# Score matmuls of a head pair on the two 64-row halves of TensorE, in a sliding-window attention with a multiplicative FFN

## The chip, the cores and the metric

One NeuronCore of one Trainium2 chip. The metric is the device time of one execution in microseconds (us), the median of several runs. Lower is better.

## What is computed

The reference runs attention over 8 batches, 8 heads, 576 positions and 64 values a head, with a causal window of 64 positions, and feeds the result to a feed-forward network whose hidden part is a product of two projections:

```python
scores = scale * np.matmul(q, k.transpose(0, 1, 3, 2))
rel = pos[:, None] - pos[None, :]
mask = (rel >= 0) & (rel < 64)
scores = np.where(mask, scores, -1e9)
scores = scores - np.max(scores, axis=-1, keepdims=True)
attn = np.exp(scores); attn = attn / (np.sum(attn, axis=-1, keepdims=True) + 1e-09)
attn_out = np.matmul(attn, v)
x = attn_out.transpose(0, 2, 1, 3).reshape(4608, 512)
a = x @ w1; b = x @ w2              # 512 -> 1024 each
out = ((a * b) @ w3) @ w_out        # 1024 -> 1024 -> 512
```

Inputs and output are float32; the kernel works in float16 with float32 accumulation.

## The kernel before, in words

**Weights.** `w3 @ w_out` is folded once into `wc_sb` (`fold_t`, `fold_mm`), so that the FFN is two projections (`ffn_ab`, L385) and one output matmul (`ffn_o`, L410). There are 9 groups of 512 tokens; each has 8 `ffn_ab` steps (two projections of 4 matmuls of 512 columns, cut in two where the ring of `xT` wraps) and 4 `ffn_o` steps (8 matmuls each).

**Attention.** Heads are taken in pairs: head `2j` lies on partitions 0 to 63 and head `2j+1` on 64 to 127 (`NJ` = 4 pairs). For each batch, Q and K are loaded by SyncE, cast to float16 (`cast_qk`), and transposed on TensorE in three chunks `c` of six 128x128 tiles (`transposes`, L246; the transposes are at L255, the copies out of PSUM at L262). K goes to `kT` with one copy of 128 partitions for each chunk. Q goes to `qT`, which holds for each pair two blocks: block `a` has head `a` on its 64 partitions and zeros on the other 64. The zeros are written once (L493, L494), and each chunk of Q needs two copies of 64 partitions, one on ScalarE (`a` = 0) and one on VectorE (`a` = 1).

`scores(d)` (L272) is one of six steps of a batch: three query segments `si`, two halves `jp` of the four pairs. It multiplies a 128-row block of K by the zero-padded Q of both heads at once (L282): the contraction runs over all 128 rows, of which the zeros take half. `s_ps` has two PSUM banks, one for each pair `jj`, with one buffer. ScalarE takes the exponential into `pt` (L287), and GpSimd cuts the window out of it with two `affine_select` passes (L296, L298). `values(d)` (L302) multiplies by V (L317, with columns of ones for the sums), ScalarE makes the reciprocal by logarithm and exponential (L326, L327, L329), and VectorE scales into `xT` (L332, L333).

**Order.** The order is written out by hand (a manual schedule). Lines 488 to 540 start up: loads, dummy matmuls[...] (`keep_busy`), K and Q of batch 0. Lines 542 to 566 interleave the attention of batch 0 with the fold. Lines 567 to 612 do the attention of batch 1 with FFN group 0 and prepare batch 2. From L617 on, a list of FFN steps with due times is worked through, and `tick(u)` (L362) puts scores, transposes, values, casts and loads of batches 2 to 7 between them; `late` (L341) says at which tick each chunk of the next batch is transposed. In the start-up and for batches 1 and 2 the chunks of a transpose go into spare views of `s_ps`, two in one tile, and into `tp`; later each goes into `tp`, which has one buffer.[...]

The functions that the change touches are `transposes`, `scores` and `values`, the start-up that writes the zeros, and the call for Q of batch 0.

Of the kernel before, what the change touches and what calls it, by code (L numbers as in the profile page):

```python
# [8 lines left out]
FP32 = mybir.dt.float32  # L9
FP16 = mybir.dt.float16  # L10
I32 = mybir.dt.int32
ALU = mybir.AluOpType
AF = mybir.ActivationFunctionType
PSUM = bass.MemoryType.PSUM

P = 128
SHIFT = 4.0
# [127 lines left out]
def kernel(  # L145
# [11 lines left out]
    nc = tc.nc  # L157
    B, H, S, D = q.shape
# [3 lines left out]
    scale = 1.0 / (D ** 0.5)  # L162
    NJ = H // 2
    TP, TI = 32, 18
# [7 lines left out]
    ident16 = keep.tile([P, P], FP16)  # L172
# [7 lines left out]
    const = fast.enter_context(tc.tile_pool(name="const", bufs=1))  # L180
    sb = fast.enter_context(tc.tile_pool(name="sb", bufs=2))
    ps_t = fast.enter_context(tc.tile_pool(name="ps_t", bufs=1, space=PSUM))
    ps_s = fast.enter_context(tc.tile_pool(name="ps_s", bufs=1, space=PSUM))
# [4 lines left out]
    dve_cp = nc.vector.tensor_copy  # L188
    act_cp = nc.scalar.copy
# [4 lines left out]

    v16s = [const.tile([P, 6, NJ, 4 * D], FP16, name=f"v16_{i}") for i in range(2)]

    qTs = [const.tile([P, NJ, 2, S], FP16, name=f"qT_{i}") for i in range(2)]


    raws, k16s, q16s = {}, {}, {}  # L200

# [16 lines left out]
    def cast_third(b, which, c, cp):  # L218
        t = raws[which, b]
        if c == 0:  # L220
            (k16s if which == "k" else q16s)[b] = sb.tile([P, TI, P], FP16, name=which + "16", bufs=1)
        t16 = (k16s if which == "k" else q16s)[b]
        cp(t16[:, 6 * c:6 * c + 6].rearrange("p i (hh d) -> p hh i d", hh=2),
           t[:, :, 6 * c * D:6 * c * D + 6 * D].rearrange("p hh (i d) -> p hh i d", d=D))
# [16 lines left out]
            dve_cp(vh[D:P, 1], vh[0:D, 2])  # L241


    kTs = {}

    def transposes(b, which, *cs, into=None, order=None):  # L246

        if cs[0] == 0 and which == "k":
            kTs[b] = sb.tile([P, NJ, S], FP16, name="kT")
        t16 = (k16s if which == "k" else q16s)[b]  # L250
        if into is None:
            into = [ps_t.tile([P, 6, P], FP16, name="tp")]
        for c, tp in zip(cs, into):
            for i in range(6):
                nc.tensor.transpose(tp[:, i, :], t16[:, 6 * c + i, :], ident16)  # L255

        def move(c, tp, a, cp):
            src = tp.rearrange("q i (p j) -> q j p i", p=TP)
            part = slice(0, P) if a is None else slice(a * D, a * D + D)
            dst = kTs[b] if a is None else qTs[b % 2][:, :, a, :]  # L260
            dst = dst[part].rearrange("q j (p i) -> q j p i", i=TI)
            cp(dst[:, :, :, 6 * c:6 * c + 6], src[part])  # L262

        if order is None:
            order = [(c, None, dve_cp) for c in cs] if which == "k" else \
                [(c, a, cp) for c in cs for a, cp in ((0, act_cp), (1, dve_cp))]
        for c, a, cp in order:
            move(c, into[cs.index(c)], a, cp)

    probs, lns = {}, {}  # L270

    def scores(d):  # L272
        b, r = divmod(d, 6)
        si, jp = divmod(r, 2)
        kT, qT = kTs[b], qTs[b % 2]
        seg = SEGS[si]
        w = 2 * sum(blk[2] for blk in seg)
        s_ps = ps_s.tile([P, 2, 512], FP32, name="s_ps")
        for jj in range(2):
            c0 = 0  # L280
            for (k0, q0, n, _) in seg:
                nc.tensor.matmul(s_ps[:, jj, c0:c0 + 2 * n].rearrange("k (a n) -> k a n", a=2),  # L282
                                 kT[:, 2 * jp + jj, k0:k0 + P], qT[:, 2 * jp + jj, :, q0:q0 + n],
                                 start=True, stop=True, skip_group_check=True)
                c0 += 2 * n
        pt = sb.tile([P, 2, 512], FP16, name="pt", bufs=3)
        nc.scalar.activation(pt[:, :, 0:w], s_ps[:, :, 0:w], AF.Exp, bias=-SHIFT, scale=scale)  # L287

        for (lo, hi, n, off, step) in [(0, 256, 128, 0, 0), (256, 384, 64, 64, 0)] if si == 0 else [(0, 512, 128, 64, -64)]:
            nb = (hi - lo) // (2 * n)  # L290
            sl = pt[:, :, lo:hi]
            if nb == 1:
                pat = [[0, 2], [0, 2], [1, n]]
            else:
                pat = [[0, 2], [step, nb], [0, 2], [1, n]]
            nc.gpsimd.affine_select(out=sl, in_=sl, pattern=pat, compare_op=ALU.is_ge,  # L296
                                    fill=0.0, base=off, channel_multiplier=-1)
            nc.gpsimd.affine_select(out=sl, in_=sl, pattern=[[-s, m] for s, m in pat], compare_op=ALU.is_ge,  # L298
                                    fill=0.0, base=63 - off, channel_multiplier=1)
        probs[d] = pt  # L300

    def values(d):  # L302
        b, r = divmod(d, 6)
        si, jp = divmod(r, 2)
        j0 = 2 * jp
        v16 = v16s[b % 2]
        pt = probs.pop(d)
        seg = SEGS[si]
        q_base = seg[0][1]
        o_ps = ps_v.tile([P, 2, 512], FP32, name="o_ps")  # L310
        for jj in range(2):
            first = True
            for a in range(2):
                c0 = 0
                for bi, (k0, q0, n, _) in enumerate(seg):
                    o0 = a * 192 + q0 - q_base
                    nc.tensor.matmul(o_ps[:, jj, o0:o0 + n],  # L317
                                     v16[:, si * 2 + bi, j0 + jj, a * D:a * D + P],
                                     pt[:, jj, c0 + a * n:c0 + a * n + n],
                                     start=first, stop=(bi == 1), skip_group_check=True)  # L320
                    first = False
                    c0 += 2 * n
        if jp == 0:
            lns[b, si] = sb.tile([P, NJ, 192], FP32, name="ln_s", bufs=4)
        y = lns[b, si][:, j0:j0 + 2]
        nc.scalar.activation(y[0:D], o_ps[D:P, :, 0:192], AF.Ln)  # L326
        nc.scalar.activation(y[D:P], o_ps[0:D, :, 192:384], AF.Ln)  # L327
        r = sb.tile([P, 2, 192], FP32, name="r")
        nc.scalar.activation(r, y, AF.Exp, scale=-1.0)  # L329
        x0 = (b * S + q_base) % RING  # L330
        xs = xT[:, j0:j0 + 2, x0:x0 + 192]
        nc.vector.tensor_tensor(xs[0:D], o_ps[0:D, :, 0:192], r[0:D], ALU.mult)  # L332
        nc.vector.tensor_tensor(xs[D:P], o_ps[D:P, :, 192:384], r[D:P], ALU.mult)  # L333
# [28 lines left out]
    def tick(u):  # L362

        b, r = divmod(u, 12)
        d = u // 2
        if u % 2 == 0 and d < ND:
            scores(d)
        ev = late.get(r, [])
        for e in ev:
            if e[0] == "t":  # L370
                event(b, *e)
        if u % 2 == 1 and 12 <= d - 1 < ND:
            values(d - 1)
        for e in ev:
            if e[0] != "t":
                event(b, *e)
        n, m = divmod(u - LAG - 4, 4)
        if m == 3 and n >= 6:
            keep_sums(n)
# [83 lines left out]
    rows = 2 * 3 * B  # L463
# [17 lines left out]
    def keep_busy(n):  # L481

        d = ps_t.tile([P, P], FP32, name="tp")
        for _ in range(n):
            nc.tensor.matmul(d, ident16, ident16, start=True, stop=True)
# [3 lines left out]
    load_qk(0, "q")  # L489
    nc.scalar.preload_act_table_set("natural_log_exp_and_others")  # L490
    make_identity(nc, ident16)
    for qT in qTs:
        nc.vector.memset(qT[D:P, :, 0, :], 0.0)  # L493
        nc.vector.memset(qT[0:D, :, 1, :], 0.0)  # L494

    def ones_of(i):
        nc.gpsimd.memset(v16s[i].rearrange("p c j (a e) -> p (c j a) e", a=2)[:, :, D:2 * D], 1.0)  # L497
# [17 lines left out]
    def spare(pool, name):  # L515

        t = pool.tile([P, 2, 1024], FP16, name=name)
        return [t[:, i, 0:768].rearrange("p (i n) -> p i n", i=6) for i in range(2)]

    keep_busy(75)  # L520
    tps = spare(ps_s, "s_ps") + spare(ps_v, "o_ps")
    for c in range(3):
        cast_third(0, "k", c, act_cp if c == 1 else dve_cp)
    transposes(0, "k", 0, 1, 2, into=tps, order=[(0, None, dve_cp), (1, None, act_cp), (2, None, dve_cp)])
    keep_busy(10)
    for c in range(3):
        cast_third(0, "q", c, act_cp if c == 1 else dve_cp)
    tps = [tps[3], ps_t.tile([P, 6, P], FP16, name="tp"), spare(ps_s, "s_ps")[0]]
    transposes(0, "q", 0, 1, 2, into=tps, order=[(0, 0, act_cp), (1, 1, dve_cp), (2, 0, act_cp), (0, 1, dve_cp),
                                                 (1, 0, act_cp), (2, 1, dve_cp)])  # L530
    keep_busy(15)
    scores(0)
    keep_busy(10)
    scores(1)
    keep_busy(30)
    for i in range(2):
# [50 lines left out]
    for d in range(6, 11):  # L587
# [10 lines left out]
        else:  # L598
            which, hh = [("k", 0), ("k", 1), ("q", 0), ("q", 1)][d - 7]
# [19 lines left out]
    for g in range(1, NG):  # L619
        part = [lambda g=g, fc=fc: ffn_ab(g, fc) for fc in range(8)] + \  # L620
               [lambda g=g, t=t: ffn_o(g, t) for t in range(4)]
        lo = need[g]
        hi = need[g + 1] if g + 1 < NG else NU
# [57 lines left out]
```

## Time and profile before

| | |
|---|---|
| time, median of 3 runs | 299.63 us (299.23 to 300.56) |
| span of the profiled execution | 298.8 us |
| TensorE matmul busy | 275.5 us (92%) |
| VectorE busy | 198.0 us (66%) |
| ScalarE busy | 178.4 us (60%) |
| GpSimd busy | 182.3 us (61%) |
| score matmuls (L282) | 192, 27.4 us busy |
| copies of Q out of PSUM (L262) | 24 on VectorE of about 960 ns, 24 on ScalarE of about 800 ns |
| exponentials of the scores (L287) | 48, 45.6 us |
| mask passes (L296, L298) | 128, 105.9 us |

A row of the groups' table names the line, the engine, the operation and the tiles; then how often it ran, its busy time, the mean duration of one, and how long its engine had been idle before it and for whom. Matmuls are pipelined: the recorded duration of one is longer than the time until the next one starts, and it is the distance between starts that says what a matmul costs TensorE.

### The profile page before, as it was taken

Reading aid. Unit: us, or ns where it says so; the run is one execution under the profiler, and the core shown is the slowest. Engines: PE = TensorE matmul, PEld = TensorE weight load, DVE = VectorE, ACT = ScalarE, POOL = GpSimd, SP = SyncE. Lnnn points to the kernel's source line nnn. Section 1 sums busy time; section 2 is a strip of 40 time slices with the busy share of each in tenths; the row PEclk is TensorE's granted clock in tenths of the full one; section 3 lists DMA queues with packets and bytes.
Section 4 is the critical chain, followed back from the end, with each engine's and each line's share of the span. In section 5 each row is a group of like instructions: output and inputs, shape, how many; then the busy total and the mean of one; then the engine's idle time right before and its main releaser. Section 6 shows DMA issues by size and latency. Waiting matters only on the chain.

```text
span 298.8 us, 5570 instructions
## 1 busy us (share of the span) xinstructions
PE 275.5 (92%) x2062; PEld 163.3 (55%) x2062; DVE 198.0 (66%) x302; ACT 178.4 (60%) x296; POOL 182.3 (61%) x214
## 2 busy tenths in 40 slices
PE   7578989798779999999999999999999999999992
PEld 7454645444535555555555798555556555544440
DVE  6816677565866776768767866589668756545531
ACT  2523784676447757787777756487769866641300
POOL 8746994578637956698669653795696453411200
PEclk9999999999989999999999999999999999999997
DMA  6999999990184936586819480970096012002012
GB/s 249 205 178 201 279 259 243 368 78 35 72 309 202 63 53 233 193 54 128 288 76 88 139 311 3 114 112 1 0 140 84 2 71 73 0 35 110 0 50 97
DMA packets 51663, 38.82 MB, mean 130 GB/s; under 512 B 38784, under 2 KB 41856, under 8 KB 51632
## 3 DMA queue, kind: packets, MB, share of 16 engines
q0 software_dynamic: 41744, 9.96, 36.1%
q1 hardware_dynamic: 9888, 28.46, 26.1%
q8 instruction: 17, 0.28, 0.4%
q14 instruction: 14, 0.11, 0.1%
HBM read 38.80 MB, written 9.44 MB: 161 GB/s over the span
## 4 chain that ended last, share of the span: by engine, by line
PE 72%; DVE 8%; ACT 7%; issue 4%; DMA 4%; POOL 3%; POOLq 0%; ACTq 0%
PE f_ps L401 36%; PE f_ps L414 19%; PE o_ps L317 7%; PE s_ps L282 5%; DMA ab<-in_moe_w_dram 4%; PE tp L255 3%; DVE xT L333 2%; ACT ln_s L327 2%; ACT r L329 2%; PE f_ps L460 2%; POOL v L497 2%; DVE kT L262 1%; DVE qT L262 1%; DVE xT L332 1%; ACT qT L262 1%
## 5 line engine op out<-in xcount | busy, mean ns | idle before, releaser
L401 PE MATMUL f_ps<-xT,w_sb 128*128 128x512 f16 (+1 forms) x640 | 135.5, 360 | 1.6 <-ACT a_sb L406 0.9
L296 POOL TENSOR_SCALAR_AFFINE_SELECT pt<-pt 128x512 f16<-128x512 f16 (+1 forms) x64 | 52.8, 825 | 72.7 <-ACT pt L287 72.7
L401 PEld LDWEIGHTS <-w_sb 128*128 128x128 f16 x640 | 60.6, 98 | 52.6 <-issue 3.6
L414 PE MATMUL f_ps<-wc_sb,ab 128*128 128x512 f16 x288 | 67.1, 379 | 0.1
L407 DVE TENSOR_TENSOR ab<-f_ps,a_sb 128x512 f16<-128x512 f32 x72 | 49.7, 691 | 19.0 <-PE f_ps L401 15.7
L287 ACT ACTIVATE pt<-s_ps 128x1024 f16<-128x1024 f32 (+1 forms) x48 | 45.6, 950 | 24.9 <-PE s_ps L282 24.1
L298 POOL TENSOR_SCALAR_AFFINE_SELECT pt<-pt 128x512 f16<-128x512 f16 (+1 forms) x64 | 53.1, 829 | 4.4
L332 DVE TENSOR_TENSOR xT<-o_ps,r 64x384 f16<-64x384 f32 x48 | 26.4, 549 | 43.8 <-ACT r L329 43.7
L406 ACT COPY a_sb<-f_ps 128x512 f32<-128x512 f32 x72 | 41.6, 579 | 22.6 <-PE f_ps L401 22.2
L326 ACT ACTIVATE ln_s<-o_ps 64x384 f32<-64x384 f32 x48 | 23.4, 487 | 44.3 <-PE o_ps L317 44.3
L414 PEld LDWEIGHTS <-ab 128*128 128x128 f16 x288 | 27.1, 98 | 28.6 <-DVE ab L407 0.6
L235 POOL DMA_DIRECT2D v<-in_v_dram x40 | 33.9, 855 | 5.4 <-DMA ab<-in_moe_w_out_dram 3.6
L317 PEld LDWEIGHTS <-v 128*128 128x128 f16 x384 | 23.5, 98 | 18.1 <-issue 4.9
L317 PE MATMUL o_ps<-pt,v 128*128 128x128 f16 (+1 forms) x384 | 27.9, 215 | 5.7 <-DVE xT L333 4.0
L416 DVE COPY t2k<-f_ps 128x512 f32<-128x512 f32 x36 | 24.8, 691 | 9.2 <-PE f_ps L414 8.5
L282 PE MATMUL s_ps<-qT,kT 128*128 128x256 f16 x192 | 27.4, 266 | 2.4 <-DVE qT L262 2.1
L333 DVE TENSOR_TENSOR xT<-o_ps,r 64x384 f16<-64x384 f32 x48 | 26.9, 560 | 0.6
L329 ACT ACTIVATE r<-ln_s 128x384 f32<-128x384 f32 x48 | 25.1, 523 | 1.5
L282 PEld LDWEIGHTS <-kT 128*128 128x128 f16 x192 | 17.8, 99 | 12.1 <-issue 3.4
L327 ACT ACTIVATE ln_s<-o_ps 64x384 f32<-64x384 f32 x48 | 23.2, 482 | 0.6
L262 DVE COPY qT<-tp 64x768 f16<-64x768 f16 x18 | 17.3, 960 | 8.4 <-ACT qT L262 8.2
L262 DVE COPY kT<-tp 128x768 f16<-128x768 f16 x17 | 16.1, 949 | 0.3 <-PE tp L255 0.2
(62 smaller groups left out, 203.2 us busy)
## 6 DMA issues: line engine op xcount, KB each, us to landing
stage<-in_k_dram SPq DMA_DIRECT2D x16, 576.0 KB
stage<-in_q_dram SPq DMA_DIRECT2D x16, 576.0 KB
out_dram<-t2k SPq DMA_DIRECT2D x36, 256.0 KB
v<-in_v_dram POOLq DMA_DIRECT2D x32, 128.0 KB, 4.5
w_sb<-in_moe_w_dram POOLq DMA_DIRECT2D x4, 512.0 KB, 11.7
ab<-in_moe_w_out_dram POOLq DMA_DIRECT2D x1, 1024.0 KB, 9.9
ab<-in_moe_w_dram POOLq DMA_DIRECT2D x2, 512.0 KB, 12.2
xT<-in_moe_w_dram POOLq DMA_DIRECT2D x2, 512.0 KB, 16.0
```

The lines of the kernel that those rows point to most:

```text
L235: nc.gpsimd.dma_start(out=vh[lo:P, c], in_=v[b, :, s0:s0 + P - lo, :].rearrange("h s d -> s h d"))
L262: cp(dst[:, :, :, 6 * c:6 * c + 6], src[part])
L282: nc.tensor.matmul(s_ps[:, jj, c0:c0 + 2 * n].rearrange("k (a n) -> k a n", a=2), kT[:, 2 * jp + jj, k0:k0 + P], qT[:, 2 * jp + jj, :, q0: ...
L287: nc.scalar.activation(pt[:, :, 0:w], s_ps[:, :, 0:w], AF.Exp, bias=-SHIFT, scale=scale)
L296: nc.gpsimd.affine_select(out=sl, in_=sl, pattern=pat, compare_op=ALU.is_ge, fill=0.0, base=off, channel_multiplier=-1)
L298: nc.gpsimd.affine_select(out=sl, in_=sl, pattern=[[-s, m] for s, m in pat], compare_op=ALU.is_ge, fill=0.0, base=63 - off, channel_multip ...
L317: nc.tensor.matmul(o_ps[:, jj, o0:o0 + n], v16[:, si * 2 + bi, j0 + jj, a * D:a * D + P], pt[:, jj, c0 + a * n:c0 + a * n + n], start=firs ...
L333: nc.vector.tensor_tensor(xs[D:P], o_ps[D:P, :, 192:384], r[D:P], ALU.mult)
L401: nc.tensor.matmul(d[:, f * n + c0:f * n + c1], w[:, dc, (fc + f) * P:(fc + f + 1) * P], xT[:, dc, xc:xc + c1 - c0], start=first, stop=(dc ...
L406: act_cp(a_sb[:, 0:nf * n], a_ps[:, 0:nf * n])
L407: nc.vector.tensor_tensor(ab[:, fc:fc + nf, lo:hi], b_ps[:, 0:nf * n].rearrange("p (f n) -> p f n", f=nf), a_sb[:, 0:nf * n].rearrange("p ...
L414: nc.tensor.matmul(o_ps, ab[:, fc, t * P:t * P + P], wc_sb[:, fc, :], start=(fc == 0), stop=(fc == 7))
```

## The change

The zero blocks go. `qT` gets the shape of `kT`, one 128-partition copy for each chunk of Q in place of two 64-partition copies (ScalarE takes chunk 1, VectorE chunks 0 and 2; for batch 0 it is the other way round), and `qT` now comes from the rotating pool with two buffers. A score step has one matmul for each head, on the 64 partitions of that head alone, so that the two heads of a pair stand on the two halves of TensorE's rows and can run beside each other: 8 matmuls of 128 (or 64) columns with 64 rows, alternating between the halves, in place of 4 of 256 (or 128) columns with 128 rows. `s_ps` and `pt` are now ordered by head first, so that each half writes a PSUM bank of its own; the mask passes and the matmuls of `values` follow that order, over the same number of elements.

```diff
-    qTs = [const.tile([P, NJ, 2, S], FP16, name=f"qT_{i}") for i in range(2)]
...
+    def transposes(b, which, *cs, into=None, cps=None):
+        t16, dst = (k16s, kTs) if which == "k" else (q16s, qTs)
+        if cs[0] == 0:
+            dst[b] = sb.tile([P, NJ, S], FP16, name=which + "T")
...
-        def move(c, tp, a, cp):
-            src = tp.rearrange("q i (p j) -> q j p i", p=TP)
-            part = slice(0, P) if a is None else slice(a * D, a * D + D)
-            dst = kTs[b] if a is None else qTs[b % 2][:, :, a, :]
-            dst = dst[part].rearrange("q j (p i) -> q j p i", i=TI)
-            cp(dst[:, :, :, 6 * c:6 * c + 6], src[part])
-
-        if order is None:
-            order = [(c, None, dve_cp) for c in cs] if which == "k" else \
-                [(c, a, cp) for c in cs for a, cp in ((0, act_cp), (1, dve_cp))]
+        if cps is None:
+            cps = [dve_cp if which == "k" or c != 1 else act_cp for c in cs]
+        for c, tp, cp in zip(cs, into, cps):
+            cp(dst[b].rearrange("q j (p i) -> q j p i", i=TI)[:, :, :, 6 * c:6 * c + 6],
+               tp.rearrange("q i (p j) -> q j p i", p=TP))
...
-        s_ps = ps_s.tile([P, 2, 512], FP32, name="s_ps")
+        s_ps = ps_s.tile([P, 2, 2, 256], FP32, name="s_ps")
         for jj in range(2):
+            j = 2 * jp + jj
             c0 = 0
             for (k0, q0, n, _) in seg:
-                nc.tensor.matmul(s_ps[:, jj, c0:c0 + 2 * n].rearrange("k (a n) -> k a n", a=2),
-                                 kT[:, 2 * jp + jj, k0:k0 + P], qT[:, 2 * jp + jj, :, q0:q0 + n],
-                                 start=True, stop=True, skip_group_check=True)
-                c0 += 2 * n
-        pt = sb.tile([P, 2, 512], FP16, name="pt", bufs=3)
-        nc.scalar.activation(pt[:, :, 0:w], s_ps[:, :, 0:w], AF.Exp, bias=-SHIFT, scale=scale)
+                for a in range(2):
+                    half = slice(a * D, a * D + D)
+                    nc.tensor.matmul(s_ps[:, a, jj, c0:c0 + n], kT[half, j, k0:k0 + P], qT[half, j, q0:q0 + n],
+                                     start=True, stop=True, skip_group_check=True)
+                c0 += n
+        pt = sb.tile([P, 2, 2, 256], FP16, name="pt", bufs=3)
+        nc.scalar.activation(pt[:, :, :, 0:w], s_ps[:, :, :, 0:w], AF.Exp, bias=-SHIFT, scale=scale)
+
+        rows = pt.rearrange("k a j n -> k (a j) n")
+        for (lo, nb, n, off, step) in MASKS[si]:
+            sl = rows[:, :, lo:lo + nb * n]
+            pat = [[0, 4], [step, nb], [1, n]]
...
-                                     pt[:, jj, c0 + a * n:c0 + a * n + n],
+                                     pt[:, a, jj, c0:c0 + n],
...
-    for qT in qTs:
-        nc.vector.memset(qT[D:P, :, 0, :], 0.0)
-        nc.vector.memset(qT[0:D, :, 1, :], 0.0)
...
-    transposes(0, "q", 0, 1, 2, into=tps, order=[(0, 0, act_cp), (1, 1, dve_cp), (2, 0, act_cp), (0, 1, dve_cp),
-                                                 (1, 0, act_cp), (2, 1, dve_cp)])
+    transposes(0, "q", 0, 1, 2, into=tps, cps=[act_cp, dve_cp, act_cp])
```

More of the change, by code (lines that the diff above doesn't have):

```diff
@@ L241, in copy_v @@
             dve_cp(vh[D:P, 1], vh[0:D, 2])
[L244 to L250, printed above, removed]
+    kTs, qTs = {}, {}
+    def transposes(b, which, *cs, into=None, cps=None):
+        t16, dst = (k16s, kTs) if which == "k" else (q16s, qTs)
+        if cs[0] == 0:
+            dst[b] = sb.tile([P, NJ, S], FP16, name=which + "T")
         if into is None:
@@ L254, in transposes @@
             for i in range(6):
-                nc.tensor.transpose(tp[:, i, :], t16[:, 6 * c + i, :], ident16)
-        def move(c, tp, a, cp):
-            src = tp.rearrange("q i (p j) -> q j p i", p=TP)
-            part = slice(0, P) if a is None else slice(a * D, a * D + D)
-            dst = kTs[b] if a is None else qTs[b % 2][:, :, a, :]
-            dst = dst[part].rearrange("q j (p i) -> q j p i", i=TI)
-            cp(dst[:, :, :, 6 * c:6 * c + 6], src[part])
-        if order is None:
-            order = [(c, None, dve_cp) for c in cs] if which == "k" else \
-                [(c, a, cp) for c in cs for a, cp in ((0, act_cp), (1, dve_cp))]
-        for c, a, cp in order:
-            move(c, into[cs.index(c)], a, cp)
+                nc.tensor.transpose(tp[:, i, :], t16[b][:, 6 * c + i, :], ident16)
+        if cps is None:
[3 more added lines that the diff above has]
+               tp.rearrange("q i (p j) -> q j p i", p=TP))
+    MASKS = [[(0, 1, 128, 0, 0), (128, 1, 64, 64, 0)]] + 2 * [[(0, 2, 128, 64, -64)]]
     probs, lns = {}, {}
@@ L274, in scores @@
         si, jp = divmod(r, 2)
-        kT, qT = kTs[b], qTs[b % 2]
+        kT, qT = kTs[b], qTs[b]
         seg = SEGS[si]
-        w = 2 * sum(blk[2] for blk in seg)
-        s_ps = ps_s.tile([P, 2, 512], FP32, name="s_ps")
+        w = sum(blk[2] for blk in seg)
+        s_ps = ps_s.tile([P, 2, 2, 256], FP32, name="s_ps")
         for jj in range(2):
+            j = 2 * jp + jj
             c0 = 0
             for (k0, q0, n, _) in seg:
-                nc.tensor.matmul(s_ps[:, jj, c0:c0 + 2 * n].rearrange("k (a n) -> k a n", a=2),
-                                 kT[:, 2 * jp + jj, k0:k0 + P], qT[:, 2 * jp + jj, :, q0:q0 + n],
-                                 start=True, stop=True, skip_group_check=True)
-                c0 += 2 * n
-        pt = sb.tile([P, 2, 512], FP16, name="pt", bufs=3)
-        nc.scalar.activation(pt[:, :, 0:w], s_ps[:, :, 0:w], AF.Exp, bias=-SHIFT, scale=scale)
-        for (lo, hi, n, off, step) in [(0, 256, 128, 0, 0), (256, 384, 64, 64, 0)] if si == 0 else [(0, 512, 128, 64, -64)]:
-            nb = (hi - lo) // (2 * n)
-            sl = pt[:, :, lo:hi]
+                for a in range(2):
[9 more added lines that the diff above has]
+            pat = [[0, 4], [step, nb], [1, n]]
             if nb == 1:
-                pat = [[0, 2], [0, 2], [1, n]]
-            else:
-                pat = [[0, 2], [step, nb], [0, 2], [1, n]]
+                pat = [[0, 4], [1, n]]
             nc.gpsimd.affine_select(out=sl, in_=sl, pattern=pat, compare_op=ALU.is_ge,
@@ L318, in values @@
                                      v16[:, si * 2 + bi, j0 + jj, a * D:a * D + P],
-                                     pt[:, jj, c0 + a * n:c0 + a * n + n],
+                                     pt[:, a, jj, c0:c0 + n],
                                      start=first, stop=(bi == 1), skip_group_check=True)
                     first = False
-                    c0 += 2 * n
+                    c0 += n
         if jp == 0:
@@ L523 @@
         cast_third(0, "k", c, act_cp if c == 1 else dve_cp)
-    transposes(0, "k", 0, 1, 2, into=tps, order=[(0, None, dve_cp), (1, None, act_cp), (2, None, dve_cp)])
+    transposes(0, "k", 0, 1, 2, into=tps, cps=[dve_cp, act_cp, dve_cp])
     keep_busy(10)
```

## The prediction, made before the changed kernel was run

> **What bounds the kernel now.** I read the slices of the page first, for the stages:
>
> ```profile
> PE   7578989798779999999999999999999999999992
> PEclk9999999999989999999999999999999999999997
> ```
>
> A slice is 7.5 us. From slice 12 on TensorE is full; before that (0 to 86 us: start-up, fold, batch 1) it has gaps. One slice in the middle has a lowered clock. The windows around it:
>
> ```profile
> 78.00:83.40 5.40, 4.24 (x34) 2.42 (x33) 4.86 (x7) 2.27 (x5) 2.18 (x2) 1.00 0.25 91
> 83.40:86.80 3.40, 1.33 (x14) 0.83 (x12) 2.84 (x6) 2.06 (x4) 0.00 (x0) 1.00 0.93 306
> 86.80:90.20 3.40, 3.40 (x13) 1.58 (x12) 1.90 (x3) 0.91 (x2) 2.87 (x5) 0.50 1.01 377
> 100.00:190.00 90.00, 90.00 (x704) 57.20 (x703) 66.42 (x103) 62.70 (x107) 63.73 (x75) 1.00 0.63 137
> ```
>
> The columns after the length are busy time of TensorE, weight load, VectorE, ScalarE, GpSimd, then the granted clock. TensorE works 1.33 of 3.40 us, and is then granted half its clock for 3.4 us. From 100 to 190 us it is never idle. So two things count: TensorE's own time after 86 us, and the chain before. Why TensorE stops at 83.5 is in the timeline (start, length, engine):
>
> ```profile
> 80.30 0.80 ACT L262 COPY qT<-s_ps 64x768 f16<-64x768 f16 x1 [1.20 <-PE s_ps L255]
> 81.29 0.68 DVE L416 COPY t2k<-f_ps 128x512 f32<-128x512 f32 x1
> 82.00 0.96 DVE L262 COPY qT<-s_ps 64x768 f16<-64x768 f16 x1
> 83.00 0.81 ACT L262 COPY qT<-s_ps 64x768 f16<-64x768 f16 x1 [1.89 <-DVE qT L262]
> 83.84 0.96 DVE L262 COPY qT<-s_ps 64x768 f16<-64x768 f16 x1 [0.87 <-ACT qT L262]
> 84.72 0.95 DVE L262 COPY qT<-tp 64x768 f16<-64x768 f16 x1
> 85.72 0.49 PE L282 MATMUL s_ps<-qT,kT 128*128 128x256 f16 x4 [2.07 <-DVE qT L262]
> ```
>
> The copies of Q of batch 2 hand over between ScalarE and VectorE one after another, and the scores wait 2.07 us for the last.
>
> Last, the cost of a matmul, as distance between starts, on TensorE alone:
>
> ```profile
> 104.03 0.60 PE L282 MATMUL s_ps<-qT,kT 128*128 128x256 f16 x4
> 104.46 0.50 PE L255 MATMUL tp<-ident,q 128*128 128x128 f16 x6
> 104.80 1.89 PE L414 MATMUL f_ps<-wc_sb,ab 128*128 128x512 f16 x8
> ...
> 212.81 0.50 PE L317 MATMUL o_ps<-pt,v 128*128 128x128 f16 x8
> 213.15 0.81 PE L414 MATMUL f_ps<-wc_sb,ab 128*128 128x512 f16 x3
> ...
> 283.53 0.59 PE L401 MATMUL f_ps<-xT,w_sb 128*128 128x512 f16 x2
> 284.05 0.19 PE L478 MATMUL tp<-ones,okv 48*1 48x1 f32 x2
> 284.17 0.60 PE L401 MATMUL f_ps<-xT,w_sb 128*128 128x512 f16 x2
> ```
>
> Four score matmuls of 256 columns take 0.43 us (108 ns each), six transposes 0.34 (56 ns for 128 columns). The eight at 212.81 are four of 128 and four of 64 columns: 0.34 us, so 28 ns for 64 columns. Each of these has its own weight load, so loads and issue allow at least one matmul every 28 ns. The three at 284 are the only place where TensorE leaves the shape of 128 rows.
>
> [...]
>
> **The change, part by part.**
>
> *Score matmuls after 86 us.* Steps 12 to 47 lie there: 24 with 128-column blocks only, 12 (first segment) with 128 and 64. Before, a step costs 4 x 108 = 432 ns, or 2 x 108 + 2 x 56 = 328 ns. After, if the halves run together, a pair of 128 columns costs 56 + 4 = 60 ns and one of 64 columns 32 ns: 4 x 60 = 240 ns, or 2 x 60 + 2 x 32 = 184 ns. To this comes a change of mode on each side. L478 prices it: the last full matmul before it starts at 283.74 (283.53 + 0.21) and has streamed by 283.96 at 216 ns a matmul; L478 starts at 284.05, so 0.09 us in. The next full matmul starts at 284.17; the two small ones, 28 ns each at most, would have ended by 284.11: 0.06 out, and the first full one is then some 10 ns late. Together 0.16 to 0.17 us, taken as 170 ns. It is another shape and type, so I keep both ends: nothing, and a whole tail of a matmul twice (recorded 379 ns minus 216 = 163 ns, so 326). With 170: 410 ns against 432, and 354 against 328. Sum 24 x (-22) + 12 x 26 = -0.2 us. The halving is nearly eaten by the changes of mode.
>
> *Score steps before 86 us* lie in the chain's shadow: TensorE waits there for VectorE's L333 at most steps, so nothing is counted.
>
> *Q copies of batch 2.* One copy of 128 partitions costs as much as one of 64, by the copies of K (950 ns on VectorE, 813 ns on ScalarE). VectorE is free at 82.0: chunk 0 to 82.95. ScalarE's chunk 1 reads the same tile and, in the changed program's order, waits for it: 82.97 to 83.8. VectorE's chunk 2 runs beside it to 83.9. Scores start at 83.97 in place of 85.72: -1.75 us.
>
> *Q copies of batch 1.* The same at 49 us, by the timeline: VectorE is free of L407 at 49.80, chunk 0 to 50.76, chunk 1 on ScalarE to 51.6. The `a_sb` copy, now at 52.46 behind three Q copies, is done at 52.2 and not at 53.0, and the TensorE matmul that waits for it moves from 53.09 to 52.25: -0.8 us, handed on through the exponential and the masks.
>
> *The clock.* With 0.4 us of idle in place of 2.07 the window is mostly busy. In 86.8 to 90.2, 8 FFN matmuls take 3.0 us in place of 1.73, and the score step some 0.3 more: 1.6 us, of which I count 1.5, since 0.38 us of TensorE idle follows at 95.5 anyway.
>
> *Steady VectorE work.* At 203.4 TensorE waits 0.72 us for L407, behind a Q copy (198.07) and copies of V. That chunk goes to ScalarE alone: -0.4.
>
> *At no cost:* the zero writes (VectorE waits for loads until 6.6 us); Q of batch 0 (the fold waits for weights until 19.06); exponential and masks (same elements, 1019 and 1125 ns); `values` (same shapes); the pool's `qT` (reused after two batches, as before). The only new waits are ScalarE's for chunk 0, counted above, and VectorE's for TensorE where it waited for ScalarE: earlier, not later.
>
> Sum: -0.2 - 1.75 - 0.8 - 1.5 - 0.4 = -4.65, so 299.63 - 4.65 = 295.0 us.
>
> **Rivals.**
>
> *Halves don't overlap* (slower). Eight matmuls of 56 ns and 170 give 618 ns, +186; the first segment 4 x 56 + 4 x 28 + 170 = 506, +178. Sum 24 x 186 + 12 x 178 = +6.6, with the front's -4.45: 301.8 us. For it: each has a weight load between. Against: loads come every 28 ns already.
>
> *Dearer change of mode*: 326 ns makes 566 (+134) and 510 (+182): +5.4, so 300.6. For it: L478 is one column and may leave sooner.
>
> *Change of mode is free*: -192 and -144 ns give -6.3; with -4.45: 288.8. For it: L478 is also float32 and one column, which may be what costs.
>
> *The clock falls elsewhere.* With Q of batch 0 ready about 1.1 us sooner, the dummy matmuls end near 16.9 in place of 18.0, and TensorE is idle 2.1 us before the fold at 19.06, as it was at 83.5. If a window falls badly, the fold loses 1.5: 296.5.
>
> **How the numbers follow.** 0.45 for my account (295.0), 0.15 without overlap (301.8), 0.12 for the dearer change (300.6), 0.13 for the free one (288.8), 0.15 for the clock (296.5). The 301.8 and the edge of 288.8 are left out: 289.0 to 300.7. Faster by 0.5% is below 298.1: account, free change and clock, 0.73. Slower is above 301.1: no overlap, 0.15. Within 0.5%: the dearer change, 0.12.
>
> **What would show it.** Starts of the two matmuls of a pair some 4 ns apart, and a score step of 0.40 us from the last matmul before to the first after; if 0.2, the change of mode is free, if 0.6, nothing overlaps. Scores of batch 2 within 0.5 us of the matmuls before, and no half clock near 85 us. If these hold and the time doesn't fall, the front's gain was lost in a wait behind it.

## The result, and the profile after

The changed kernel takes 296.41 us (median of 4 runs, 296.17 to 297.91) against 299.84 for the kernel before on the same chip (299.23 to 300.56): a ratio of 0.9895 with a 95% interval of 0.9855 to 0.9935, so 3.1 us less, between 1.9 and 4.3 (the two medians differ by 3.4). Run once more beside the first experiments it gave 0.9867 (0.9819 to 0.9915), 4.0 us less. The two profiled executions have spans of 298.8 and 294.3 us.

The slices of the page after, TensorE and its granted clock:

```profile
PE   7758889898799999999999999999999999999992
PEclk9999999999999999999999999999999999999998
```

The lowered slice in the middle is gone. The windows around it (length; busy time of TensorE, weight load, VectorE, ScalarE, GpSimd; clock; DMA):

```profile
78.00:83.40 5.40, 4.12 (x38) 2.24 (x37) 5.32 (x8) 1.60 (x4) 1.69 (x2) 1.00 0.32 99
83.40:86.80 3.40, 3.40 (x39) 1.87 (x36) 3.05 (x7) 2.31 (x4) 2.06 (x5) 1.00 0.92 329
86.80:90.20 3.40, 3.40 (x34) 1.98 (x33) 1.42 (x3) 2.31 (x6) 3.33 (x4) 1.00 1.02 385
100.00:190.00 90.00, 90.00 (x780) 53.45 (x780) 64.62 (x100) 57.43 (x96) 61.48 (x73) 1.00 0.63 139
```

TensorE works through from 83.4 us at the full clock (1.00), where before it worked 1.33 of 3.40 us and then ran at half (0.50). Between 100 and 190 us it is full in both kernels, while ScalarE's busy time fell by 5.3 us there: relief for which TensorE doesn't wait in that stretch. The handing over of Q of batch 2 in the timeline:

```profile
79.93 0.96 DVE L257 COPY kT<-tp 128x768 f16<-128x768 f16 x1
80.94 0.49 PE L253 MATMUL tp<-ident,q 128*128 128x128 f16 x6 [1.17 <-DVE kT L257]
81.40 0.95 DVE L257 COPY qT<-s_ps 128x768 f16<-128x768 f16 x1
82.27 0.95 DVE L257 COPY qT<-tp 128x768 f16<-128x768 f16 x1
82.39 0.81 ACT L257 COPY qT<-s_ps 128x768 f16<-128x768 f16 x1 [3.77 <-DVE qT L257]
83.27 0.34 PE L278 MATMUL s_ps<-qT,kT 64*128 64x128 f16 x8
```

As worked out: chunk 0 on VectorE, then chunks 1 and 2 beside each other, and the scores at 83.27 in place of 85.72. Last, a score step on TensorE alone, once with 128-column blocks only and once of the first segment:

```profile
99.04 1.03 PE L395 MATMUL f_ps<-xT,w_sb 128*128 128x512 f16 x4
100.00 0.40 PE L278 MATMUL s_ps<-qT,kT 64*128 64x128 f16 x8
100.33 0.51 PE L253 MATMUL tp<-ident,q 128*128 128x128 f16 x6
100.68 0.81 PE L408 MATMUL f_ps<-wc_sb,ab 128*128 128x512 f16 x3
...
205.86 0.34 PE L278 MATMUL s_ps<-qT,kT 64*128 64x128 f16 x8
206.14 0.51 PE L253 MATMUL tp<-ident,k 128*128 128x128 f16 x6
```

The starts of the single matmuls in that trace, in us, are these (h is the half, by the order of the program):

```
99.690  FFN matmul, 512 columns (has streamed at 99.906)
100.002 h0   100.005 h1
100.068 h0   100.071 h1
100.123 h0   100.127 h1
100.179 h0   100.183 h1
100.331 first transpose   100.397 second   100.453 third
```

Each FFN matmul is recorded with 379 ns there and follows the one before it at 216; the score matmuls are recorded with 216 to 226. The two matmuls of a pair start 3 to 4 ns apart, and the pairs follow at 56 ns (66 after the first): by these records the halves overlap. But TensorE waits 96 ns before the first (from 99.906, which is the start of the FFN matmul and the 216 ns at which such matmuls follow one another, to 100.002), 92 ns after the last (100.183 + 0.056 to 100.331), and the second transpose is 10 ns late (66 in place of 56). These are what the two changes of mode, from 128 rows to 64 and back, cost in this step. From the end of the FFN matmul to the first transpose a step takes 425 ns, and 10 more are lost behind it: 435 against 436 before. In the first segment it is 372 and 10, against 330.

**Where the time went, by stage.** Two executions don't start alike (the fold begins when its weights have landed, at 19.06 us before and 19.71 after), so I compare distances between the starts of score steps, counted from 0 (six a batch, 48 in all), in the traces:

| us | step 2 at | 2 to 6 | 6 to 12 | 12 to 14 | 14 to 47 | 47 to end |
|---|---|---|---|---|---|---|
| before | 26.06 | 27.89 | 31.77 | 6.80 | 165.64 | 40.65 |
| after | 26.78 | 26.85 | 29.64 | 5.23 | 165.26 | 40.53 |
| difference | +0.72 | -1.04 | -2.13 | -1.57 | -0.38 | -0.12 |

Steps 6 and 12 are the first of batches 1 and 2. Of 5.2 us gained behind step 2, 4.7 come from the two hand-overs of Q and the clock behind the second, and 0.5 from all the rest, in which 33 score steps with the new matmuls lie.

### The profile page after: what moved, and what is told of

Same layout as the page of the kernel before. It is cut to its first block, busy times and chain, and to the rows that moved or that the text cites. A ratio compares the mean times of both kernels' runs of the same rounds, so it can differ in the third digit from the quotient of the medians.

```text
span 294.3 us, 5925 instructions
## 1 busy us (share of the span) xinstructions
PE 274.1 (93%) x2254; PEld 152.9 (52%) x2254; DVE 185.4 (63%) x289; ACT 168.4 (57%) x281; POOL 180.8 (61%) x214
## 4 chain that ended last, share of the span: by engine, by line
PE 76%; DVE 6%; ACT 5%; DMA 4%; issue 3%; POOL 3%; POOLq 0%; DVEq 0%; ACTq 0%
PE f_ps L395 38%; PE f_ps L408 19%; PE o_ps L311 7%; PE tp L253 5%; DMA ab<-in_moe_w_dram 4%; PE s_ps L278 4%; DVE xT L327 2%; PE f_ps L454 2%; ACT ln_s L321 2%; ACT r L323 2%; POOL v L488 2%; DVE kT L257 1%; DVE xT L326 1%; ACT ln_s L320 1%; ACT pt L282 1%
## 5 line engine op out<-in xcount | busy, mean ns | idle before, releaser
L395 PE MATMUL f_ps<-xT,w_sb 128*128 128x512 f16 (+1 forms) x640 | 134.1, 358 | 0.0
L290 POOL TENSOR_SCALAR_AFFINE_SELECT pt<-pt 128x512 f16<-128x512 f16 (+1 forms) x64 | 52.1, 814 | 69.0 <-ACT pt L282 68.9
L395 PEld LDWEIGHTS <-w_sb 128*128 128x128 f16 x640 | 59.7, 98 | 50.7 <-issue 0.5
L292 POOL TENSOR_SCALAR_AFFINE_SELECT pt<-pt 128x512 f16<-128x512 f16 (+1 forms) x64 | 52.4, 819 | 4.4
L278 PEld LDWEIGHTS <-kT 64*128 64x128 f16 x384 | 10.5, 94 | 16.5 <-issue 14.8
L278 PE MATMUL s_ps<-qT,kT 64*128 64x128 f16 (+1 forms) x384 | 18.2, 214 | 0.3 <-ACT pt L282 0.2
L454 PE MATMUL f_ps<-ab,t2k 128*128 128x512 f16 x64 | 15.0, 379 | 0.4 <-DVE t2k L448 0.3
```

Of the source, the lines that this page charges most:

```text
L278: nc.tensor.matmul(s_ps[:, a, jj, c0:c0 + n], kT[half, j, k0:k0 + P], qT[half, j, q0:q0 + n], start=True, stop=True, skip_group_check=True)
L395: nc.tensor.matmul(d[:, f * n + c0:f * n + c1], w[:, dc, (fc + f) * P:(fc + f + 1) * P], xT[:, dc, xc:xc + c1 - c0], start=first, stop=(dc ...
```

## The experiments

The theory, A: the gain is the single copy of Q, by what it takes off the chain at batches 1 and 2; the halves break even because each step changes the mode of TensorE twice. Rival B: the halves bring the gain. Rival D: it is relief of VectorE and ScalarE, spread over all batches.

**The halves alone.** The kernel before, with its zero-padded Q, its two copies and its zero writes:

```diff
-        s_ps = ps_s.tile([P, 2, 512], FP32, name="s_ps")
+        s_ps = ps_s.tile([P, 2, 2, 256], FP32, name="s_ps")
...
+                    nc.tensor.matmul(s_ps[:, a, jj, c0:c0 + n], kT[half, j, k0:k0 + P], qT[half, j, a, q0:q0 + n],
```

> The kernel before with the score matmuls alone changed: two matmuls of 64 rows on the two halves, reading the two blocks of the zero-padded Q, scores ordered by head; the two copies of each Q chunk and the zero writes stay. Theory A (the gain comes from the Q copies alone, the halves only break even because each step changes the mode of TensorE twice): 36 steps after 86 us at 425 and 372 ns in place of 436 and 330, so +0.2 us, about 300.0 where before is 299.8, and the idle 2.07 us before the scores of batch 2 and the half clock are still there. Theory B (the halves bring the gain): about 296.4, -3.4 us.

Measured 301.41 us against 300.69: ratio 1.0026 (1.0006 to 1.0045). The halves alone gain nothing and cost a little: B has fallen. In the stage from step 14 to 47 its trace has 166.00 us against 165.64: +0.36, which is the price of the halves where TensorE is full (10 first-segment steps at +52 ns and 23 others at -1 ns make +0.5).

**The copies alone.** The kernel before with the new `transposes`, and matmuls of 128 rows as before; since there are no zero blocks it multiplies 2n neighbouring columns of Q and doesn't keep the two heads apart:

```diff
-                                 kT[:, 2 * jp + jj, k0:k0 + P], qT[:, 2 * jp + jj, :, q0:q0 + n],
+                                 kT[:, 2 * jp + jj, k0:k0 + P], qT[:, 2 * jp + jj, x:x + 2 * n],  # x = min(q0, S - 2 * n)
```

> The other part alone: one copy of 128 partitions for each Q chunk and no zero blocks, but score matmuls as before, 4 of all 128 rows and 256 (or 128) columns. It reads 2n neighbouring columns of Q, so the two heads of a pair are not kept apart in it; everything else runs as in the kernel before. Theory A: the changed kernel's gain or 0.2 us more, about 296.2. Theory B: about 299.8. Theory C (both parts are needed, half each): about 298.

295.93 us, ratio 0.9849 (0.9798 to 0.9901): all of the gain of the changed kernel, so C, which needs both parts, has fallen too. By the medians it is 0.5 us more, which the intervals can't tell. Its stages from step 2 to 47, as in the table: 26.85, 29.79, 5.13, 164.76. The first three are those of the changed kernel to 0.15 us; the fourth is 0.88 less than before, and 0.50 less than with the halves. All of the 0.88 lies between steps 35 and 36, where the wait near 203 us was.

**The clock.** The kernel before, with 8 dummy matmuls in the idle stretch of TensorE ahead of the scores of batch 2:

```diff
+            if u == 24:
+                fill = ps_v.tile([P, 2, 512], FP32, name="o_ps")
+                for _ in range(8):
+                    nc.tensor.matmul(fill[:, 0, :], ident16, wc_sb[:, 0, :], start=True, stop=True)
             tick(u)
```

> The kernel before with 8 dummy matmuls of 512 columns (1.73 us, into a free PSUM tile) in the idle stretch of TensorE before the scores of batch 2. They end before Q is ready, so nothing else moves. If the half clock at 86.8 us follows from that idle stretch, it goes: -1.5 us, about 298.3, and no slice of lowered clock in the middle. If the half clock has another cause[...], it stays and the time is 299.8 or above.

299.52 us, ratio 0.9964 (0.9942 to 0.9986): 1.1 us faster by doing more. The windows of this kernel, in the same columns:

```profile
83.40:86.80 3.40, 3.05 (x22) 1.66 (x21) 2.70 (x5) 2.06 (x4) 0.00 (x0) 1.00 0.94 299
86.80:90.20 3.40, 3.40 (x24) 1.87 (x23) 3.11 (x4) 2.08 (x4) 2.71 (x5) 1.00 1.01 362
```

The half clock is gone, and steps 12 to 14 take 5.12 us in place of 6.80; nothing else moved (27.90, 31.77, 165.64). So here the half clock followed from the idle stretch: 0.50 behind 1.33 us of work, 1.00 behind 3.05. The mean is 1.1 and not 1.5 us (0.4 to 1.7 by the interval). In the trace of the halves alone TensorE also idles about 2 us there, and no half clock follows:

```profile
83.40:86.80 3.40, 2.22 (x14) 1.01 (x13) 2.50 (x4) 1.50 (x4) 0.00 (x0) 1.00 0.43 116
86.80:90.20 3.40, 2.33 (x21) 1.31 (x22) 3.28 (x7) 1.79 (x4) 0.73 (x2) 1.00 0.96 340
```

What stood ahead of a half clock can be read from the traces. In that of before the granted clock is full for 81.92 us, half for 3.41, full again for 204.80 and then half; in that of the changed kernel it is full for 286.72 us and then half. The full stretches are 24, 60 and 84 times the 3.413 us of the half one, so I divided both traces into stretches of that length and summed TensorE's recorded matmul time in each. In before two have half clock behind them, with 39% (83.37 to 86.78 us) and 41% (291.58 to 294.99, at the end of the work); in the changed kernel it is the last at full clock, with 11% (288.10 to 291.51). All the others at full clock have 53% or more, and full clock behind them. Two stretches between these values, from the kernels with two copies for batch 2 and with longer dummies that come below, each with the one behind it:

```profile
15.54:18.95 3.41, 1.60 (x29) 1.42 (x26) 0.00 (x0) 0.66 (x1) 0.70 (x1) 1.00 1.52 189
18.95:22.37 3.42, 2.56 (x23) 1.60 (x24) 1.29 (x2) 0.00 (x0) 2.55 (x4) 1.00 1.90 165
...
10.37:13.79 3.42, 1.54 (x24) 1.39 (x25) 2.79 (x4) 2.83 (x4) 2.86 (x4) 1.00 1.10 168
13.79:17.20 3.41, 3.41 (x41) 2.73 (x39) 0.00 (x0) 0.97 (x2) 0.28 (x1) 0.50 1.18 206
```

So 1.60 of 3.41 us (47%) had full clock behind it, and 1.54 of 3.42 (45%) had half. In the kernel before, the idle stretch of batch 2 left 1.33 of 3.40 us and cost a second time; in the halves alone it left 2.22 and 2.33 of 3.40 us and didn't. More than these cases is not shown.

**The changed kernel again**, beside these three:

> The changed kernel again, beside these three on the same chip: about 296.4, -3.4 us from before. The profile pair gave -4.5; if that is the mean over more runs, 295.3.

296.45 us, ratio 0.9867: 4.0 us, between the first comparison and the profile pair.

**Is the overlap of the halves real?** First by order: the loop over the heads outermost, four matmuls of one half and then four of the other.

```diff
-        for jj in range(2):
-            j = 2 * jp + jj
-            c0 = 0
-            for (k0, q0, n, _) in seg:
-                for a in range(2):
+        for a in range(2):
+            half = slice(a * D, a * D + D)
+            for jj in range(2):
+                j = 2 * jp + jj
+                c0 = 0
+                for (k0, q0, n, _) in seg:
```

> The changed kernel with the loop over the two heads outermost, so that four matmuls of one half follow one another before the other half has its turn; the same 8 matmuls, the same two changes of mode. If the overlap of the halves is real, only one pair of neighbours can overlap: a step then takes some 7 x 56 and the two changes of 96 and 92 ns, 580 ns in place of 425 (first segment 450 in place of 372): 24 x 155 + 12 x 80 = +4.7 us, about 301 where the changed kernel has 296.4. If the overlapping starts in the records are only an image of the recorder and the halves run in turn anyway, nothing moves: 296.4.

296.63 us, ratio 0.9860 (0.9808 to 0.9912): nothing moved that can be told. My expectation failed, and by itself that looks like the second reading. The starts of the single matmuls in its trace, for a step with 128-column blocks only, and for one of the first segment with the columns of each:

```
105.797 FFN matmul, 512 columns
106.108 106.122   106.174 106.187   106.230 106.243   106.286 106.299
106.447 first transpose
...
110.788 128   110.802 128      110.855 64   110.867 64
110.883 128   110.896 128      110.940 64   110.952 64
```

Again pairs, now 13 ns apart. The columns of the second step show more: the program has 128, 64, 128, 64 for one half and then the same for the other, but the starts on record come as 128, 128, 64, 64 and again. That isn't the order of the program, by which I had worked out the 301 us. Then the counter-test: both heads on the lower 64 rows, so that nothing can overlap (the upper head's scores are those of the lower one's).

```diff
-                    half = slice(a * D, a * D + D)
+                    half = slice(0, D)
```

> The changed kernel with both heads of a pair on the lower 64 rows (the upper head's data are not used, so its scores are those of the lower head): the same 8 matmuls of 64 rows, the same changes of mode, but one half only. If two halves work at the same time in the changed kernel, here they can't: a step takes 8 x 56 ns and 188 for the two changes, 636 in place of 425 (first segment 524 in place of 372): 24 x 211 + 12 x 152 = +6.9 us over the changed kernel, 303.3. If matmuls of 64 rows are simply quicker, nothing moves: 296.4.

303.79 us, ratio 1.0129 (1.0074 to 1.0185), as expected; 7.3 us above the changed kernel with longer dummies (296.48) on the same chip. TensorE alone in its timeline:

```profile
99.75 1.89 PE L395 MATMUL f_ps<-xT,w_sb 128*128 128x512 f16 x8
101.57 0.62 PE L278 MATMUL s_ps<-qT,kT 64*128 64x128 f16 x8
102.12 0.51 PE L253 MATMUL tp<-ident,q 128*128 128x128 f16 x6
```

From 101.57 to 102.12 are 0.55 us, against 0.33 (100.00 to 100.33) with two halves; a whole step, counted as above, takes 645 ns against 425. So 64 rows by themselves are not quicker, and the overlap is real: two halves take 220 ns a step less than one. For the kernel with the halves in turn, whose step took 435 ns, I estimate the same: with 188 ns for the two changes, the 645 ns on one half leave some 57 for each of eight matmuls, so two that start 13 ns apart would be of different halves. The records name neither the half of a matmul nor its place in the queue, and where the order of these starts comes from is not shown.

**Which batches.** The changed kernel with Q copied by two copies of 64 partitions for some batches only, first batch 2, then batches 3 to 7:

```diff
+        if which == "q" and b == 2:          # the second kernel: b > 2
+            for c, tp in zip(cs, into):
+                for lo, cp in ((0, act_cp), (D, dve_cp)):
+                    cp(dst[b][lo:lo + D].rearrange("q j (p i) -> q j p i", i=TI)[:, :, :, 6 * c:6 * c + 6],
+                       tp[lo:lo + D].rearrange("q i (p j) -> q j p i", p=TP))
+            return
```

> The changed kernel with Q of batch 2 alone copied by two copies of 64 partitions for each chunk, as before (ScalarE then VectorE). Theory A: the scores of batch 2 start some 1.8 to 2 us later, and in the executions where a clock window covers the idle stretch some 1.6 us more is lost: +1.8 to +3.4 from the changed kernel, 298.2 to 299.8. Rival D (the gain is spread over all batches as relief of VectorE and ScalarE): +0.5 at most, 296.9.

> The same for batches 3 to 7 and not for batch 2: the stage where TensorE is always busy. Theory A: only the wait of 0.6 to 0.7 us near 203 us comes back, with what other small waits there are: +0.7 to +0.9 from the changed kernel, 297.2. Rival D: +2.5 or more, 298.9.

Batch 2: 299.39 us, ratio 0.9944 (0.9924 to 0.9965), 2.8 us above the kernel with the halves in turn (296.63), its neighbour: it ran beside it on the same chip. Most of the gain is lost with this one batch. Its timeline has the old hand-over again:

```profile
81.31 0.96 DVE L259 COPY qT<-s_ps 64x768 f16<-64x768 f16 x1
82.30 0.81 ACT L259 COPY qT<-s_ps 64x768 f16<-64x768 f16 x1 [1.89 <-DVE qT L259]
83.14 0.96 DVE L259 COPY qT<-s_ps 64x768 f16<-64x768 f16 x1 [0.88 <-ACT qT L259]
84.03 0.95 DVE L259 COPY qT<-tp 64x768 f16<-64x768 f16 x1
85.03 0.33 PE L284 MATMUL s_ps<-qT,kT 64*128 64x128 f16 x7 [0.64 <-DVE qT L259]
```

Steps 6 to 14 take 36.83 us against 34.87: +1.96, in an execution without a half clock. The rest of the 2.8 is probably the clock in others: of the 22 executions 8 took 297.8 to 298.7 us and 14 took 299.0 to 300.3, but only one has a trace. Batches 3 to 7: 297.16 us, ratio 0.9870 (0.9818 to 0.9922), 0.5 us above its neighbour; in the trace steps 14 to 47 take 166.02 us against 165.26. So D has fallen but for this part, and all of it lies between steps 35 and 36 again. No run changed batch 1 alone; its part rests on the stages of the traces.

**Going on along the same path.** In the hand-over after the change TensorE waits 1.17 us for VectorE's copy of the third K chunk, while ScalarE has nothing to do. The changed kernel with that copy of batches 1 and 2 on ScalarE:

```diff
-    transposes(1, "k", 2)
+    transposes(1, "k", 2, cps=[act_cp])
...
-    transposes(2, "k", 2)
+    transposes(2, "k", 2, cps=[act_cp])
```

> The changed kernel with the third K chunk of batches 1 and 2 copied by ScalarE, which is idle then, and not by VectorE, whose queue holds it up: for batch 2 the last six transposes of Q wait 1.17 us for that copy, in the single buffer. Theory A (what is left on the path ahead of 86 us is the queue of copies): transposes of the third Q chunk follow those of the first two at once, Q is ready 1 to 1.5 us sooner for batch 2 and some 0.3 for batch 1: -1.3 to -1.8, about 294.9. If another wait takes its place there: 296.4.

295.80 us, ratio 0.9837 (0.9791 to 0.9882), 0.8 us below its neighbour, about half of what I expected. The timeline:

```profile
78.49 0.79 ACT L257 COPY kT<-tp 128x768 f16<-128x768 f16 x1
79.58 0.50 PE L253 MATMUL tp<-ident,q 128*128 128x128 f16 x6
79.90 0.69 DVE L410 COPY t2k<-f_ps 128x512 f32<-128x512 f32 x1
80.50 0.94 DVE L257 COPY qT<-s_ps 128x768 f16<-128x768 f16 x1
82.37 0.34 PE L278 MATMUL s_ps<-qT,kT 64*128 64x128 f16 x8 [0.57 <-DVE qT L257]
```

The wait of TensorE is gone and the transposes are 1.36 us sooner, but VectorE's queue holds the Q copy until 80.50, behind two scalings of `xT` and an output copy. The scores gain 0.87 us (step 6 to 12: 28.77 in place of 29.64). Batch 1 gains nothing in this trace: step 2 to 6 takes 27.19 us against 26.85. Another execution with the same edit, in the last kernel below, has 26.75, so the 27.19 needn't come from the edit.

**More dummies at the start.** Half clock at the start (about 21 to 24.5 us) was in the traces of three kernels: the halves alone, the copies alone, and two copies for the late batches; sixteen matmuls of the fold took 5.30 and 5.31 us in the first two, against 3.63 with the longer dummies below. So 65 dummies in place of 30 ahead of the fold, alone and with the K copies:

```diff
-    keep_busy(30)
+    keep_busy(65)
```

> The changed kernel with 65 dummy matmuls in place of 30 ahead of the fold, so that TensorE idles some 0.3 to 0.8 us there and not 2.2 to 2.7. Half clock at the start was seen in three profiles (21 to 24.4 us) of kernels with that wait. If it comes from the idle stretch, it can't come any more: the same as the changed kernel in executions without it, and the mean some 0.3 to 0.8 lower, about 295.9; never a slice of lowered clock near 21 us. If the dummies run into the fold, slower by up to 0.3.

> Both additions to the changed kernel: the third K chunk of batches 1 and 2 on ScalarE, and the 65 dummy matmuls. -0.7 to -1.0 for the first, as measured, and -0.3 to -0.8 for the second: about 295.1. If the second brings nothing, 295.6.

296.48 us (0.9882, 0.9840 to 0.9924) and 295.43 us (0.9848, 0.9805 to 0.9891), against 0.9867 to 0.9895 and 0.9837 without: no gain that can be told. In both traces half clock begins at 13.4 or 13.8 us, ahead of the 65 dummies. The matmuls before them take longer in it (ten dummies 1.23 and 1.25 us, against 0.72 at that place in the copies alone), so that the 65 start at about 17 us and hold TensorE until the fold begins behind them, at 20.8 and 20.7, past the time (about 19.5) at which the weights were there in other executions. The longer dummies don't cause this half clock: the kernel with both heads on one half, from the same chip and with 30 dummies, has it from 13.2 to 20.1 us, and its fold begins at 20.6. In all three traces the 3.41 us ahead, from about 10 us, have TensorE at 35 to 45%. So half clock came here ahead of the stretch that the dummies fill, and no trace shows the longer dummies without the earlier one. The K copies on ScalarE alone, at 295.80 us, can't be told from both additions, at 295.43.

## Why the prediction was right, and where its sizes were off

The forecast was 295.0 us, 4.65 less; measured are 3.1 in the first comparison (1.9 to 4.3) and 4.0 in the second. Direction and mechanism hold. That the sum came so near is in part luck: its terms are off by 0.2 to 0.8 us in both directions. Step by step:

- *Score matmuls after 86 us*, forecast -0.2 us: +0.4 to +0.6, a small loss where a small gain was forecast. The mechanism is right, down to the two changes of mode: 96 ns in for the 90 read from L478, 92 out for the 60, and 10 behind it as read. The 4 ns added for the second matmul of a pair stood on no trace then; in the trace after, the starts of a pair are 3 to 4 ns apart, and the four pairs take 237 ns (100.002 to 100.183 + 0.056) for the forecast's 240. The term that was mis-sized is the way out; with it the two changes cost 198 ns a step and not 170. L478, with one column and no 128-column weight load, was a good model of the way in and a poor one of the way out.
- *Q copies of batch 2*, forecast -1.75: -2.13 in the profile pair, -1.96 with only that batch changed back. VectorE came to chunk 0 some 0.3 us sooner, counted from step 6, than the 82.0 us taken.
- *Q copies of batch 1*, forecast -0.8: -1.04. In the second profile of the changed kernel it is -0.39 (27.50 us), since Q's load landed 0.55 us later than ScalarE wanted it; so this part isn't had in each execution.
- *The clock*, forecast -1.5: -1.57 in the profile pair, but -1.1 over executions (0.4 to 1.7). Here the step was wrong in kind: it took what one trace showed as certain. That less idling leaves no half clock was my estimate then; the dummy matmuls bear it out for this stretch (1.00 in place of 0.50). Much the same idle stretch left 1.33 of 3.40 us and then a clock of 0.50 in one trace, and 2.22 of 3.40 us and then 1.00 in another. A loss that comes in a part of the executions is worth its mean.
- *Steady VectorE work*, forecast -0.4: the copies alone gain 0.88 in steps 14 to 47, and two copies for the late batches cost 0.76 there. The wait near 203 us is gone, and it is the whole of both numbers; the forecast had half of it.
- *At no cost*: exponentials and masks have the same durations (949 and 817 ns a call on average against 950 and 827). Q of batch 0 is ready sooner and the fold doesn't start sooner, as said.
- The rival *clock falls elsewhere* came true in part: half clock at the start is in several traces, but also in one with the old copies of Q (the halves alone, after 1.94 us of idle), so the change is not needed for it. Of the traces with 30 dummies it lies behind the wait for the fold's weights in two of eight with the new copies of Q of batch 0 and in one of three with the old: too few to tell whether it comes more often with the change.

Added up, the trace's stages give -5.2 us behind step 2, and the later start of the fold gives 0.7 back; that start differs between executions of like kernels (19.06 to 20.09 us over the traces in which it waits for the weights), by when the weights land. The runs moved by less than the 4.5 us of the profile pair, 3.1 and 4.0 us. The clock (0.4 short of the forecast) and the halves (0.6 to 0.8 dearer) point that way, the steady part (0.5 more) and batch 2 the other; with intervals of over a microsecond on each side these can't be divided further, and the division above rests on the traces.

## What to carry to other kernels

Splitting the score matmuls onto two halves of the rows didn't pay here: against the zero-padded matmuls about 200 ns were saved and 198 paid for the two changes of mode at each step, and the shorter steps of the first segment saved 146 and lost 52. So before splitting a matmul, set what the packed work between two changes saves against the changes. Before working on an engine that is full, look for the places where it stops: two hand-overs of some microseconds ahead of the full stretch, with the clock behind the second, were worth 4.7 us of the trace's 5.2, more than 36 matmul groups in it, and behind an idle stretch of 2 us the half clock cost 1.6 us again in the trace of before. Copies of one PSUM tile that alternate between two engines ran one after the other here (82.00, 83.00 and 83.84 us before), while copies of two tiles ran beside each other (82.27 and 82.39 us after the change); a copy of 128 partitions cost the same as one of 64 (0.95 and 0.96 us on VectorE).

## What the runs showed of the hardware that was not expected

- In the kernel with the halves in turn the starts on record were not in the order of the program: with four matmuls of one half ahead of four of the other in the program, they come in pairs 13 ns apart, in a first-segment step as 128, 128, 64, 64 columns where the program has 128, 64, 128, 64. Its step took 435 ns, against 425 when the halves alternate and 645 when all are on one half.
- In the trace of the changed kernel the change from 128 to 64 rows cost 96 ns in, 92 ns out and 10 ns behind, the same to a few ns in all 35 steps after 84 us, with FFN matmuls or those of `values` before them and transposes or FFN matmuls behind.
- Half clock came behind stretches that were far from idle: behind 1.54 of 3.42 us with longer dummies (45%) and 1.33 of 3.40 before (39%), while 1.60 of 3.41 us with two copies for batch 2 (47%) had full clock behind it. What brings the full clock back is not shown.
